# A fused attention and two-layer feed-forward kernel: the second product in seven chunks of 512 tokens

## The chip, the cores and the metric

The kernel runs on one core of a Trainium2 chip. The metric is the device time of one execution in microseconds (us): the median of the runs, and lower is better. The times shown for the kernel before are 1512.82, 1510.32 and 1512.70 us, so the median is 1512.7.

## The reference

Attention over 8 batches, 12 heads, 448 tokens and 64 dimensions, with a root-mean-square norm on queries and keys, and behind it a feed-forward network with h·cos(h) as its activation. All is float32.

```python
def _attn_ref(q, k, v, g_q, g_k):            # each (8, 12, 448, 64)
    q_n, k_n = rmsnorm(q, g_q), rmsnorm(k, g_k)
    scores = scale * np.matmul(q_n, k_n.transpose(0, 1, 3, 2))
    attn = softmax(scores)
    return np.matmul(attn, v)

def _moe_ref(x, w_in, w_out):                # (3584, 768), (768, 2048), (2048, 768)
    h = x @ w_in
    g = h * np.cos(h)
    return g @ w_out

x = attn_out.transpose(0, 2, 1, 3).reshape(8 * 448, 12 * 64)
```

## The kernel before

Everything is kept transposed: features lie on the 128 partitions, tokens along the row. One batch has 448 tokens (`S`), and 8 batches (`B`) make 3584.

The kernel has two parts, each with its own plan. A `Plan` is a list scheduler in the kernel's source: every step is added with its engine, an assumed cost, a due time and the buffers that it reads and writes, and `order()` plays the steps through by these figures and gives the order in which they are issued. On the chip each engine takes its instructions in that order and waits on semaphores for what they need.

The first part does the attention for all batches (two heads at a time), and between its steps the first product, h = x·w_in, for batches 0 to 6 (`multiply`, `ffn1`, lines L545 to L547). There are 16 blocks (`fc`) of 128 rows of h. Each is the sum over six slices of the 768 features, and each slice takes three matmuls, because x and the weights are split into a rounded high part and the rest: high·high, high·low and low·high. So a block is 18 matmuls of 128x128 weights on 448 columns. ScalarE copies a finished block out of PSUM (`h_out`, L557), and SyncE (SP) stores it to DRAM in `h_d` (`h_store`, L560). The weights of the second product are split in the same way and lie in DRAM in `wo_d`.

The second part does the first product of the last batch (`ffn1_block`), and behind it the second product for all batches, one batch of 448 tokens after the other. In the order of the instructions on the chip the last splits of x of the first part (`x_split`, L529 and L531) stand between the first steps of the second part. While the last batch's blocks run, each weight tile of the first product is replaced by one of the second (`v_place`). The second product goes through the 16 blocks of h in pairs (`NG = 2`):

- `gl_load` (L567): SP loads a pair of blocks of one batch from `h_d` into `hb`, 128 x 2 x 448. The ring has 4 buffers.
- `g_turns` (L574 on VectorE, L576 on GpSimd): the whole turns of 2π in h, times -C1. The ring `n` has 2 buffers.
- `g_reduce` (L582, L584 on VectorE): h less these turns. The ring `r2` has 2 buffers.
- `g_cos` (L588, L589 on ScalarE): the absolute value, and the sine of π/2 less it.
- `g_mul` (L593 on VectorE): times h.
- `g_split` (L602 on ScalarE, L600 on GpSimd): the high part and the rest, three buffers each.
- `ffn2` (L616 to L618 on TensorE): for each of the two blocks, into each of six PSUM banks (one for 128 of the 768 output features), three matmuls of 128x128 weights on 448 columns, 18 in all.

A chunk holds its six banks over all 16 blocks. There are eight banks in the ring, so the next chunk starts on the two that are free, and then needs those that were just finished. `y_out` copies a bank to SBUF (ScalarE L630 for even `oc`, VectorE L632 for odd ones, and the very last bank in two halves), and `y_store` (L635) stores it on SP's queue. SBUF slots for these copies are those of `xf`, one for each of the six heads' pairs of the attention part.

Of the kernel before, what the change touches and what calls it, by code (L numbers as in the profile page):

```python
# [10 lines left out]
F32 = mybir.dt.float32  # L11
F32R = mybir.dt.float32r
# [12 lines left out]
PE, ACT, DVE, POOL, SP = "PE", "ACT", "DVE", "POOL", "SP"  # L25


class Plan:
# [18 lines left out]
    def add(self, eng, cost, due, fn, *args, r=(), w=(), land=0.0, start=0.0, lead=None):  # L47
        n = len(self.parts)
        deps = set()
        for key in r:  # L50
            deps.update(self.writer.get(key, ()))
        for key in w:
            deps.update(self.writer.get(key, ()))
            deps.update(self.readers.get(key, ()))
        for key in (*r, *w):
            name, inst = key[0], key[1]
            if name in self.rings:
                self.users.setdefault((name, inst), []).append(n)
        for key in r:
            self.readers.setdefault(key, []).append(n)  # L60
        for key in w:
            self.writer[key] = [n]
            self.readers[key] = []
        deps.discard(n)
        self.parts.append((eng, cost, due, fn, args, deps, land))
        self.start.append(start)
        self.lead.append(self.LEAD * (eng == PE) if lead is None else lead)
# [59 lines left out]
def tile_attention_moe(  # L127
# [11 lines left out]
    nc = tc.nc  # L139
    NU = sd_in.shape[0]  # L140
    B, S, D = 8, kT.shape[2], 64
# [7 lines left out]
    NFC = w_in.shape[0]  # L149
    NOC = 6  # L150
    DM = NCC * 128
    HM = DM // 2
    f64 = w_in.dtype == mybir.dt.int64
    NG = 2


    cpool = ctx.enter_context(tc.tile_pool(name="cpool", bufs=1))
    wpool = ctx.enter_context(tc.tile_pool(name="wpool", bufs=1))
    xpool = ctx.enter_context(tc.tile_pool(name="xpool", bufs=1))
    epool = ctx.enter_context(tc.tile_pool(name="epool", bufs=2))  # L160
    dpool = ctx.enter_context(tc.tile_pool(name="dpool", bufs=1, space=bass.MemoryType.DRAM))
# [4 lines left out]
    ps_o = att.enter_context(tc.tile_pool(name="ps_o", bufs=1, space=PSUM))  # L166
    ps_h = att.enter_context(tc.tile_pool(name="ps_h", bufs=1, space=PSUM))

    h_d = dpool.tile([B, NFC, 128, S], F32, tag="h_d", name="h_d")
    wo_d = dpool.tile([NFC, 128, 2, DM], F32, tag="wo_d", name="wo_d")  # L170
    rk_d = dpool.tile([NU, 128, 7], F32, tag="rk_d", name="rk_d")
    rs_d = dpool.tile([NU, 7, 128], F32, tag="rs_d", name="rs_d")
# [329 lines left out]
    xf = {}  # L502
# [50 lines left out]
    hes = {}  # L553
# [3 lines left out]
        nc.scalar.copy(he, phs.pop((b, fc))[:, :S])  # L557

    def h_store(b, fc):
        nc.sync.dma_start(h_d[b, fc], hes.pop((b, fc)))  # L560


    gts = {}

    def gl_load(b, gi):
        hb = gpool.tile([128, NG, S], F32, tag="hb", name=f"hb{b}_{gi}", bufs=4)
        nc.sync.dma_start(hb, h_d[b, gi * NG : gi * NG + NG].rearrange("f p s -> p f s"))  # L567
        gts[(b, gi)] = {"h": hb}

    def g_turns(b, gi, step):  # L570
        d = gts[(b, gi)]
        if step == 0:
            n = d["n"] = gpool.tile([128, NG, S], F32, tag="n", name=f"n{b}_{gi}", bufs=2)
            nc.vector.tensor_scalar(n, d["h"], 1.0 / (2.0 * math.pi), MAGIC, op0=ALU.mult, op1=ALU.add)  # L574
        else:
            nc.gpsimd.tensor_scalar(d["n"], d["n"], -MAGIC, -C1, op0=ALU.add, op1=ALU.mult)  # L576

    def g_reduce(b, gi, step):
        d = gts[(b, gi)]
        if step == 0:  # L580
            r = d["r"] = gpool.tile([128, NG, S], F32, tag="r2", name=f"r2{b}_{gi}", bufs=2)
            nc.vector.tensor_tensor(r, d["h"], d["n"], ALU.add)  # L582
        else:
            nc.vector.scalar_tensor_tensor(d["r"], d.pop("n"), C2 / C1, d["r"], op0=ALU.mult, op1=ALU.add)  # L584
# [9 lines left out]

    def g_split(b, gi, lo):
        d = gts[(b, gi)]
        t = gpool.tile([128, NG, S], F32R, tag="glo" if lo else "ghi", name=f"g{lo}{b}_{gi}")
        d["lo" if lo else "hi"] = t
        if lo:
            nc.gpsimd.tensor_tensor(t, d.pop("r"), d["hi"].bitcast(F32), ALU.subtract)  # L600
        else:
            nc.scalar.copy(t, d["r"])  # L602

    ys = {}

    def ffn2(b, fc):
        d = gts[(b, fc // NG)]
        hi, lo = d["hi"][:, fc % NG, :], d["lo"][:, fc % NG, :]
        w = wts[("wo", fc)]
        for oc in range(NOC):  # L610
            if fc == 0:
                ys[(b, oc)] = ps_y.tile([128, 512], F32, tag="y", name=f"y{b}_{oc}")
            y = ys[(b, oc)][:, :S]
            whi = w[:, 0, oc * 128 : oc * 128 + 128]
            wlo = w[:, 1, oc * 128 : oc * 128 + 128]
            nc.tensor.matmul(y, whi, hi, start=(fc == 0), stop=False)  # L616
            nc.tensor.matmul(y, whi, lo, start=False, stop=False)  # L617
            nc.tensor.matmul(y, wlo, hi, start=False, stop=(fc == NFC - 1))  # L618

    yes = {}  # L620

    def y_out(b, oc, hf=None):
        y = ys[(b, oc)][:, :S]
        if (b, oc) not in yes:
            yes[(b, oc)] = xpool.tile([128, S], F32, tag=f"xf{oc}", name=f"ye{b}_{oc}")
        ye = yes[(b, oc)]
        if hf is not None:
            y, ye = (t[:, hf * S // 2 : hf * S // 2 + S // 2] for t in (y, ye))
        if (hf if hf is not None else oc) % 2 == 0:
            nc.scalar.copy(ye, y)  # L630
        else:
            nc.vector.tensor_copy(ye, y)  # L632

    def y_store(b, oc):
        nc.sync.dma_start(out[oc * 128 : oc * 128 + 128, b * S : (b + 1) * S], yes.pop((b, oc)))  # L635


    plan = Plan(RING)
    add = plan.add
    ISS, LAND = 0.45, 5.0  # L640
# [159 lines left out]
    def multiply(b):  # L800
        for fc in range(NFC):
            key = ("ph", NSP + NFC * b + fc)
            for part in range(3):
                d = ffn_due(b, 3 * fc + part)
                r = [("w", fc), ("wlo", fc, 0), ("wlo", fc, 1)]
                r += [("xs", cc, s) for cc in (2 * part, 2 * part + 1) for s in range(2)]
                add(PE, 1.215, d, ffn1, b, fc, part, ps_h, "ph", r=r, w=[key])
            add(ACT, 0.53, d - 4, h_out, b, fc, r=[key], w=[("he", NFC * b + fc)])
            add(SP, ISS, d, h_store, b, fc, r=[("he", NFC * b + fc)], land=LAND)
# [22 lines left out]
    gpool = ctx.enter_context(tc.tile_pool(name="gpool", bufs=3, reuse_waits="tile"))  # L832
    ps_y = ctx.enter_context(tc.tile_pool(name="ps_y", bufs=8, space=PSUM, reuse_waits="tile"))
    plan = Plan(RING2)
    add = plan.add
    BLOCK = 3.66

    for fc in range(NFC):
        d = BLOCK * fc
        add(PE, BLOCK, d, ffn1_block, B - 1, fc, w=[("y", fc), ("w", fc)])  # L840
        add(ACT, 0.53, d + 4.0, h_out, B - 1, fc, r=[("y", fc)], w=[("he", fc)])
        add(SP, ISS, d + 5.0, h_store, B - 1, fc, r=[("he", fc)], w=[("hd", B - 1, fc)], land=LAND)
        add(SP, ISS, d + 6.0, v_place, fc, w=[("w", fc)], land=8.0)
    for b in range(B):
        for gi in range(NFC // NG):
            n = (NFC // NG) * b + gi
            d = BLOCK * (NFC * (b + 1) + NG * gi)
            hb, t, r2, hi, lo = (("hb", n), ("n", n), ("r2", n), ("ghi", n), ("glo", n))
            add(SP, ISS, d - 30.0, gl_load, b, gi, r=[("hd", b, NG * gi + i) for i in range(NG)], w=[hb], land=LAND)
            add(DVE, 0.9, d - 20.0, g_turns, b, gi, 0, r=[hb], w=[t])  # L850
            add(POOL, 1.3, d - 19.0, g_turns, b, gi, 1, w=[t])
            add(DVE, 1.1, d - 17.0, g_reduce, b, gi, 0, r=[hb, t], w=[r2])
            add(DVE, 1.8, d - 16.0, g_reduce, b, gi, 1, r=[t], w=[r2])
            add(ACT, 2.0, d - 14.0, g_cos, b, gi, w=[r2])
            add(DVE, 1.12, d - 11.0, g_mul, b, gi, r=[hb], w=[r2])
            add(ACT, 0.95, d - 9.0, g_split, b, gi, 0, r=[r2], w=[hi])
            add(POOL, 2.8, d - 8.0, g_split, b, gi, 1, r=[r2, hi], w=[lo])
            for fc in (NG * gi, NG * gi + 1):
                out_keys = [("y", NFC + NOC * b + oc) for oc in range(NOC)]
                add(PE, BLOCK, BLOCK * (NFC * (b + 1) + fc), ffn2, b, fc, r=[hi, lo, ("w", fc)], w=out_keys)  # L860
        for oc in range(NOC):
            y = ("y", NFC + NOC * b + oc)
            d = BLOCK * NFC * (b + 2) + oc
            if b == B - 1 and oc == NOC - 1:
                add(ACT, 0.3, d - 12.0, y_out, b, oc, 0, r=[y], w=[("ye", oc)])
                add(DVE, 0.35, d - 12.0, y_out, b, oc, 1, r=[y], w=[("yf", oc)])
            else:
                add(DVE if oc % 2 else ACT, 0.62 if oc % 2 else 0.53, d - 12.0, y_out, b, oc, r=[y], w=[("ye", oc)])
            add(SP, ISS, d, y_store, b, oc, r=[("ye", oc), ("yf", oc)], land=LAND)
    with tc.manual_schedule():  # L870
        for f, a in plan.order():
# [48 lines left out]
```

## Time and profile before

| what | value |
|---|---|
| median of the 3 runs shown (lowest, highest) | 1512.7 us (1510.32, 1512.82) |
| span of the profiled execution | 1515.6 us |
| busy: TensorE, its weight loads, VectorE, ScalarE, GpSimd | 1469.8, 1224.4, 1049.0, 874.2, 856.5 us |
| granted TensorE clock, mean | 0.993 |
| matmuls of the second product | 3 lines of 768 |
| DMA traffic | 204.33 MB, mean 135 GB/s |

The profiled execution has no other time of its own than its span, which is 2.9 us (0.2%) over the median. PE is TensorE's matmuls and PEld its weight loads, which run beside them; DVE is VectorE, ACT ScalarE, POOL GpSimd, and SPq the DMA issues of SyncE's queue. Matmuls are pipelined: the recorded duration of one is longer than the distance to the start of the next, and a busy TensorE isn't one at its peak. A wait is put down to the releaser that came last.

### The profile page before, as it was taken

The numbers are of one execution on the slowest core, as the hardware profiler recorded it, in microseconds if no ns is written. First come the engines' busy times: TensorE is split into PE (matmuls) and PEld (weight loads), VectorE is DVE, ScalarE is ACT, GpSimd is POOL, SyncE is SP. The second block draws the span as 40 slices with busy tenths as digits, with TensorE's granted clock in tenths as the row PEclk, the third lists the DMA queues.
The fourth block names the chain that finished last, engine by engine and source line by source line (L and its number), as shares of the span: only waits on it lengthen the run. The fifth ranks groups of instructions, "written<-read, shape, count | busy, mean of one in ns | idle before, by whom it ended". The sixth has DMA issues, their size and how long they took to land.

```text
span 1515.6 us, 22459 instructions
## 1 busy us (share of the span) xinstructions
PE 1469.8 (97%) x7692; PEld 1224.4 (81%) x7692; DVE 1049.0 (69%) x1891; ACT 874.2 (58%) x1763; POOL 856.5 (57%) x694
## 2 busy tenths in 40 slices
PE   7898998999999999999999999999999999999998
PEld 3446787878788878877877788789999999999998
DVE  7878998778777777777776765451566666566561
ACT  5767777677767766766765665441344344344441
POOL 5869788766856655865755552131444444544441
PEclk9999999999999999999999999999999999999999
DMA  6577424555545455544444431296133233233221
GB/s 205 179 217 218 123 82 132 182 177 172 157 155 184 144 152 164 162 147 144 150 153 126 130 118 57 67 310 218 60 100 107 62 97 98 61 99 104 66 74 37
DMA packets 116963, 204.33 MB, mean 135 GB/s; under 512 B 19232, under 2 KB 95856, under 8 KB 116848
## 3 DMA queue, kind: packets, MB, share of 16 engines
q1 hardware_dynamic: 116848, 202.90, 42.9%
q8 instruction: 60, 0.98, 0.3%
q14 instruction: 55, 0.45, 0.1%
HBM read 149.55 MB, written 53.29 MB: 134 GB/s over the span
## 4 chain that ended last, share of the span: by engine, by line
PE 78%; DVE 6%; ACT 3%; issue 3%; POOL 1%; DMA 0%; ACTq 0%; POOLq 0%; DVEq 0%
PE y L616 10%; PE y L618 10%; PE y L617 10%; PE ph L545 9%; PE ph L546 8%; PE ph L547 8%; PE O L500 8%; PE PT L464 7%; PE S L419 6%; ACT hi L475 1%; DVE lo L483 1%; DVE S L426 1%; DVE xf L517 1%; DVE hi L485 1%; ACT P L439 0%
## 5 line engine op out<-in xcount | busy, mean ns | idle before, releaser
L545 PE MATMUL ph<-xs,wi 128*128 128x448 f32 x768 | 299.5, 390 | 3.5 <-ACT he L557 3.5
L546 PE MATMUL ph<-xs,wi 128*128 128x448 f32 x768 | 282.7, 368 | 0.9 <-DVE xs L531 0.9
L547 PE MATMUL ph<-xs,wi 128*128 128x448 f32 x768 | 281.6, 367 | 0.0
L616 PE MATMUL y<-g,wo 128*128 128x448 f32 x768 | 281.1, 366 | 0.0
L618 PE MATMUL y<-g,wo 128*128 128x448 f32 x768 | 280.8, 366 | 0.0
L617 PE MATMUL y<-g,wo 128*128 128x448 f32 x768 | 280.7, 366 | 0.0
L439 ACT ACTIVATE P<-S,sm 128x448 f32<-128x448 f32 x336 | 214.4, 641 | 99.7 <-DVE S L426 88.9
L600 POOL TENSOR_TENSOR g<-r,g 128x896 fp32r<-128x896 f32 x64 | 139.6, 2181 | 184.9 <-ACT g L602 184.9
L426 DVE TENSOR_SCALAR_CACHE_REDUCE S<-S,nr 128x448 f32<-128x448 f32 x336 | 219.4, 683 | 19.0 <-PE S L419 17.5
L475 ACT CAST hi<-PT 128x448 fp32r<-128x448 f32 x336 | 164.8, 536 | 86.5 <-PE PT L464 47.7
L483 DVE TENSOR_TENSOR lo<-PT,hi 128x448 fp32r<-128x448 f32 x252 | 145.3, 617 | 79.7 <-ACT hi L475 78.9
L464 PEld LDWEIGHTS PT<-ident,P 128*128 128x128 f32 x1344 | 158.6, 143 | 33.9 <-issue 22.8
L464 PE MATMUL PT<-ident,P 128*128 128x128 f32 x1344 | 184.2, 278 | 0.1
L545 PEld LDWEIGHTS ph<-xs,wi 128*128 128x128 f32 x768 | 145.2, 189 | 34.9 <-issue 12.9
L547 PEld LDWEIGHTS ph<-xs,wi 128*128 128x128 f32 x768 | 145.0, 189 | 12.5
L616 PEld LDWEIGHTS y<-g,wo 128*128 128x128 f32 x768 | 144.2, 188 | 13.1 <-ACT ye L630 0.7
L546 PEld LDWEIGHTS ph<-xs,wi 128*128 128x128 f32 x768 | 145.5, 189 | 10.9 <-DVE xs L531 1.6
L618 PEld LDWEIGHTS y<-g,wo 128*128 128x128 f32 x768 | 144.2, 188 | 11.9
L617 PEld LDWEIGHTS y<-g,wo 128*128 128x128 f32 x768 | 144.2, 188 | 11.6
L582 DVE TENSOR_TENSOR r<-hb,n 128x896 f32<-128x896 f32 x64 | 93.1, 1455 | 84.9 <-POOL g L600 82.2
L297 POOL TENSOR_TENSOR r<-r,nhalf 128x14 f32<-128x14 f32 (+1 forms) x50 | 127.2, 2545 | 42.8 <-DVE r L293 32.7
L593 DVE TENSOR_TENSOR r<-r,hb 128x896 f32<-128x896 f32 x64 | 73.3, 1146 | 101.8 <-ACT r L589 101.8
(83 smaller groups left out, 2545.2 us busy)
## 6 DMA issues: line engine op xcount, KB each, us to landing
h_d<-he SPq DMA_DIRECT2D x128, 224.0 KB
hb<-h_d SPq DMA_DIRECT2D x64, 448.0 KB
sd<-sd SPq DMA_DIRECT2D x46, 448.0 KB
vd<-v SPq DMA_DIRECT2D x84, 160.0 KB
qd<-qT SPq DMA_DIRECT2D x48, 256.0 KB
raw<-w_in SPq DMA_DIRECT2D x16, 768.0 KB
rawo<-w_out SPq DMA_DIRECT2D x32, 384.0 KB
wo_d<-rawo SPq DMA_DIRECT2D x32, 384.0 KB
```

What stands on the lines that cost most here:

```text
L426: nc.vector.tensor_scalar(d["S", t][:, :S], d["S", t][:, :S], d["nr"][:, t : t + 1], None, op0=ALU.mult, op1=ALU.min, accum_out=d["sm"][:, ...
L439: nc.scalar.activation(tl(u, f"P{t}", [128, S], F32, "P"), d.pop(("S", t))[:, :S], AF.Exp, bias=sm[:, 1, t : t + 1], scale=-1.0, accum_out ...
L464: nc.tensor.transpose(pt[:, t * 128 : t * 128 + 128], src, ident)
L475: nc.scalar.copy(hi, pt[:, hh * S : hh * S + S])
L483: nc.vector.tensor_tensor(lo, src, hi.bitcast(F32), ALU.subtract)
L545: nc.tensor.matmul(ph[:, :S], whi, x2[:, 0, :], start=(cc == 0), stop=False)
L546: nc.tensor.matmul(ph[:, :S], whi, x2[:, 1, :], start=False, stop=False)
L547: nc.tensor.matmul(ph[:, :S], wlo, x2[:, 0, :], start=False, stop=(cc == NCC - 1))
L600: nc.gpsimd.tensor_tensor(t, d.pop("r"), d["hi"].bitcast(F32), ALU.subtract)
L616: nc.tensor.matmul(y, whi, hi, start=(fc == 0), stop=False)
L617: nc.tensor.matmul(y, whi, lo, start=False, stop=False)
L618: nc.tensor.matmul(y, wlo, hi, start=False, stop=(fc == NFC - 1))
```

## The change

The second product takes its tokens in seven chunks (`NT`) of 512 columns (`CT`), not in eight batches of 448. A chunk goes across the borders of batches, and so `h_d` in DRAM is laid out as 16 blocks of 128 rows of 3584 tokens: a store of one batch's block writes 128 pieces of 1792 bytes that lie 14336 bytes apart, and a load reads pieces of 2048 bytes. All tiles of the pair's steps are 512 wide, a matmul fills a whole PSUM bank, and the copies of the result have six slots of their own (`ye`), not those of `xf`. The planner's figures for the second part are changed to fit.

```diff
+    CT = 512
+    NT = B * S // CT
-    h_d = dpool.tile([B, NFC, 128, S], F32, tag="h_d", name="h_d")
+    h_d = dpool.tile([NFC, 128, B * S], F32, tag="h_d", name="h_d")
...
     def h_store(b, fc):
-        nc.sync.dma_start(h_d[b, fc], hes.pop((b, fc)))
+        nc.sync.dma_start(h_d[fc][:, b * S : b * S + S], hes.pop((b, fc)))
...
     def gl_load(b, gi):
-        hb = gpool.tile([128, NG, S], F32, tag="hb", name=f"hb{b}_{gi}", bufs=4)
-        nc.sync.dma_start(hb, h_d[b, gi * NG : gi * NG + NG].rearrange("f p s -> p f s"))
+        hb = gpool.tile([128, NG, CT], F32, tag="hb", name=f"hb{b}_{gi}", bufs=4)
+        nc.sync.dma_start(hb, h_d[gi * NG : gi * NG + NG, :, b * CT : b * CT + CT].rearrange("f p s -> p f s"))
...
-            n = d["n"] = gpool.tile([128, NG, S], F32, tag="n", name=f"n{b}_{gi}", bufs=2)
+            n = d["n"] = gpool.tile([128, NG, CT], F32, tag="n", name=f"n{b}_{gi}", bufs=2)
...
-            r = d["r"] = gpool.tile([128, NG, S], F32, tag="r2", name=f"r2{b}_{gi}", bufs=2)
+            r = d["r"] = gpool.tile([128, NG, CT], F32, tag="r2", name=f"r2{b}_{gi}", bufs=2)
...
-        t = gpool.tile([128, NG, S], F32R, tag="glo" if lo else "ghi", name=f"g{lo}{b}_{gi}")
+        t = gpool.tile([128, NG, CT], F32R, tag="glo" if lo else "ghi", name=f"g{lo}{b}_{gi}")
...
-            y = ys[(b, oc)][:, :S]
+            y = ys[(b, oc)]
...
-            yes[(b, oc)] = xpool.tile([128, S], F32, tag=f"xf{oc}", name=f"ye{b}_{oc}")
+            yes[(b, oc)] = gpool.tile([128, CT], F32, tag=f"ye{oc}", name=f"ye{b}_{oc}", bufs=1)
...
-    BLOCK = 3.66
+    BLOCK, BLOCK2 = 3.66, 4.1
+    D2 = BLOCK * NFC
...
-    for b in range(B):
+    for b in range(NT):
         for gi in range(NFC // NG):
             n = (NFC // NG) * b + gi
-            d = BLOCK * (NFC * (b + 1) + NG * gi)
+            d = D2 + BLOCK2 * (NFC * b + NG * gi)
+            bs = range(b * CT // S, (b * CT + CT - 1) // S + 1)
...
-                add(PE, BLOCK, BLOCK * (NFC * (b + 1) + fc), ffn2, b, fc, r=[hi, lo, ("w", fc)], w=out_keys)
+                add(PE, BLOCK2, D2 + BLOCK2 * (NFC * b + fc), ffn2, b, fc, r=[hi, lo, ("w", fc)], w=out_keys)
```

The assumed costs of the pair's steps change with the width too (for instance L600 on GpSimd from 2.8 to 2.5 us, L602 on ScalarE from 0.95 to 1.08), and so do the widths in `y_out` and `y_store`.

More of the change, by code (lines that the diff above doesn't have):

```diff
@@ L622, in y_out @@
     def y_out(b, oc, hf=None):
-        y = ys[(b, oc)][:, :S]
+        y = ys[(b, oc)]
         if (b, oc) not in yes:
-            yes[(b, oc)] = xpool.tile([128, S], F32, tag=f"xf{oc}", name=f"ye{b}_{oc}")
+            yes[(b, oc)] = gpool.tile([128, CT], F32, tag=f"ye{oc}", name=f"ye{b}_{oc}", bufs=1)
         ye = yes[(b, oc)]
         if hf is not None:
-            y, ye = (t[:, hf * S // 2 : hf * S // 2 + S // 2] for t in (y, ye))
+            y, ye = (t[:, hf * CT // 2 : hf * CT // 2 + CT // 2] for t in (y, ye))
         if (hf if hf is not None else oc) % 2 == 0:
@@ L634, in y_store @@
     def y_store(b, oc):
-        nc.sync.dma_start(out[oc * 128 : oc * 128 + 128, b * S : (b + 1) * S], yes.pop((b, oc)))
+        nc.sync.dma_start(out[oc * 128 : oc * 128 + 128, b * CT : (b + 1) * CT], yes.pop((b, oc)))
     plan = Plan(RING)
@@ L843, in tile_attention_moe @@
         add(SP, ISS, d + 6.0, v_place, fc, w=[("w", fc)], land=8.0)
-    for b in range(B):
+    for b in range(NT):
         for gi in range(NFC // NG):
             n = (NFC // NG) * b + gi
-            d = BLOCK * (NFC * (b + 1) + NG * gi)
+            d = D2 + BLOCK2 * (NFC * b + NG * gi)
+            bs = range(b * CT // S, (b * CT + CT - 1) // S + 1)
             hb, t, r2, hi, lo = (("hb", n), ("n", n), ("r2", n), ("ghi", n), ("glo", n))
[L849 to L857, printed above, removed]
+            add(SP, ISS, d - 30.0, gl_load, b, gi, r=[("hd", bb, NG * gi + i) for i in range(NG) for bb in bs], w=[hb], land=LAND)
+            add(DVE, 1.0, d - 20.0, g_turns, b, gi, 0, r=[hb], w=[t])
+            add(POOL, 1.5, d - 19.0, g_turns, b, gi, 1, w=[t])
+            add(DVE, 1.66, d - 17.0, g_reduce, b, gi, 0, r=[hb, t], w=[r2])
+            add(DVE, 1.3, d - 16.0, g_reduce, b, gi, 1, r=[t], w=[r2])
+            add(ACT, 2.3, d - 14.0, g_cos, b, gi, w=[r2])
+            add(DVE, 1.3, d - 11.0, g_mul, b, gi, r=[hb], w=[r2])
+            add(ACT, 1.08, d - 9.0, g_split, b, gi, 0, r=[r2], w=[hi])
+            add(POOL, 2.5, d - 8.0, g_split, b, gi, 1, r=[r2, hi], w=[lo])
@@ L858, in tile_attention_moe @@
             for fc in (NG * gi, NG * gi + 1):
                 out_keys = [("y", NFC + NOC * b + oc) for oc in range(NOC)]
-                add(PE, BLOCK, BLOCK * (NFC * (b + 1) + fc), ffn2, b, fc, r=[hi, lo, ("w", fc)], w=out_keys)
+                add(PE, BLOCK2, D2 + BLOCK2 * (NFC * b + fc), ffn2, b, fc, r=[hi, lo, ("w", fc)], w=out_keys)
         for oc in range(NOC):
             y = ("y", NFC + NOC * b + oc)
-            d = BLOCK * NFC * (b + 2) + oc
-            if b == B - 1 and oc == NOC - 1:
+            d = D2 + BLOCK2 * NFC * (b + 1) + oc
@@ L865, in tile_attention_moe @@
+            if b == NT - 1 and oc == NOC - 1:
                 add(ACT, 0.3, d - 12.0, y_out, b, oc, 0, r=[y], w=[("ye", oc)])
@@ L867, in tile_attention_moe @@
             else:
-                add(DVE if oc % 2 else ACT, 0.62 if oc % 2 else 0.53, d - 12.0, y_out, b, oc, r=[y], w=[("ye", oc)])
+                add(DVE if oc % 2 else ACT, 0.7 if oc % 2 else 0.6, d - 12.0, y_out, b, oc, r=[y], w=[("ye", oc)])
             add(SP, ISS, d, y_store, b, oc, r=[("ye", oc), ("yf", oc)], land=LAND)
```

## The prediction

> **What bounds the kernel now.** I read the page's busy line, its slices and its chain first, then the second product's part of the trace by windows, then its waits.
>
> ```profile
> span 1515.6 us, 22459 instructions
> PE 1469.8 (97%) x7692; PEld 1224.4 (81%) x7692; DVE 1049.0 (69%) x1891; ACT 874.2 (58%) x1763; POOL 856.5 (57%) x694
> ...
> PE y L616 10%; PE y L618 10%; PE y L617 10%; PE ph L545 9%; PE ph L546 8%; PE ph L547 8%; PE O L500 8%; PE PT L464 7%; PE S L419 6%; ACT hi L475 1%; DVE lo L483 1%; DVE S L426 1%; DVE xf L517 1%; DVE hi L485 1%; ACT P L439 0%
> ...
> L616 PE MATMUL y<-g,wo 128*128 128x448 f32 x768 | 281.1, 366 | 0.0
> ```
>
> TensorE is the bound, and the three lines of the second product (L616 to L618) carry 10% of the chain each. 366 ns is the recorded life of one matmul, not its price: neighbours overlap. The price is the distance from one start to the next, so I take windows of one chunk each (core 0, TensorE alone: us, busy and count, clock, DMA share, GB/s).
>
> ```profile
> 1043.04:1102.56 59.52, 59.52 (x289) 1.00 0.23 71
> 1102.56:1160.94 58.38, 58.38 (x289) 1.00 0.29 93
> 1160.94:1219.32 58.38, 58.38 (x289) 1.00 0.26 82
> ...
> 1453.10:1511.62 58.52, 58.52 (x289) 1.00 0.12 41
> sum 468.58, PE 468.58; mean PE 58.57
> ```
>
> Eight chunks of 288 matmuls (the 289th is the neighbour's), no idle time, full clock: 58.38 / 288 = 202.7 ns a matmul in an ordinary chunk, 59.52 / 288 = 206.7 ns in the first. The stage takes 468.6 us, and almost nothing else is in it. From 1043 us on TensorE's own waits are these:
>
> ```profile
> PEld y L616 <- ACT ye L630: 0.7, 3, 0.2
> ```
>
> That is three stops at chunk borders, where the evacuation of a bank came late. So the stage's time is a count of matmuls times a spacing, and the question is what 512 columns do to the spacing.
>
> **The change part by part.** The count first. 16 blocks x 18 matmuls x 7 chunks = 2016 in place of 2304, 288 fewer. The columns in all are the same, 2016 x 512 = 2304 x 448. Only what a matmul costs beside its columns can be saved.
>
> The price of a column comes from a stretch in which the clock was halved (a window, then the list of instructions in it: start, life).
>
> ```profile
> 125.90:132.60 6.70, 5.76 (x19) 0.50 0.41 123
> ...
> 130.21 0.57 PE L546 MATMUL ph<-xs,wi 128*128 128x448 f32 x1
> ...
> 132.08 0.57 PE L500 MATMUL O<-hi,vs 128*128 128x448 f32 x1
> ```
>
> Five spacings in 132.08 - 130.21 = 1.87 us: 374 ns for 448 columns, 0.835 ns a column at clock 0.50. At full clock that is 187 ns for 448 columns and 213.5 for 512. The measured 202.7 is 16 ns more, and in the first chunk 20 ns more. What are they? They don't come from the next matmul's weight load: a matmul with no load behind it lives as long.
>
> ```profile
> 607.49 0.37 PE L546 MATMUL ph<-xs,wi 128*128 128x448 f32 x1
> 607.49 0.19 PEld L547 LDWEIGHTS ph<-xs,wi 128*128 128x128 f32 x1
> 607.70 0.37 PE L547 MATMUL ph<-xs,wi 128*128 128x448 f32 x1
> 607.99 0.19 PEld L419 LDWEIGHTS S<-khi,qhi 64*128 64x128 f32 x2 [0.31 <-issue]
> ```
>
> The matmul of 607.70 lives its neighbour's 0.37 us, though no load starts in the 0.29 us after it. All matmuls of this form in the trace have 448 columns, so no row shows how the 16 ns go with the width. Bounds: they vanish in a longer stream (spacing 213.5), they stay (229.5), or they grow with the columns (202.7 x 512/448 = 231.6). I take the fixed one, 229.5: two spacings stand in the trace for the same 448 columns, 202.7 and 206.7, so the excess follows something other than the columns, and at half clock the spacing grows 1.85 times, not twice, so it doesn't run on the array's clock. The rows leave the third nearly as open, at 2 ns from it. Sum: 2016 x 229.5 = 462.7 us against 468.6: **-5.9**.
>
> A rule to weigh here: the Trainium skill's "TensorE: Matmul & The Clock Gate", section "Back-to-back issue gap", gives N / 2.4 + 2.5 ns for a warm matmul, which is 189 ns at 448 columns and 216 at 512. The trace disagrees at 448 by 14 ns; by the rule at 512 alone, the estimate for the stage is 435 us. The section "Wait — 56ns, not 53.3ns?" of that page says that the fixed part does not show on the cold array; the 374 ns agree.
>
> Elementwise work on h, in groups of the steady stage (mean ns after the busy time):
>
> ```profile
> L600 POOL TENSOR_TENSOR g<-r,g 128x896 fp32r<-128x896 f32 x53 | 114.4, 2159 | 131.6 <-ACT g L602 131.6
> L582 DVE TENSOR_TENSOR r<-hb,n 128x896 f32<-128x896 f32 x51 | 76.0, 1491 | 48.0 <-POOL g L600 48.0
> L576 POOL TENSOR_SCALAR n<-n 128x896 f32<-128x896 f32 x50 | 67.4, 1347 | 71.0 <-DVE n L574 69.3
> L593 DVE TENSOR_TENSOR r<-r,hb 128x896 f32<-128x896 f32 x52 | 59.7, 1149 | 81.1 <-ACT r L589 81.1
> L584 DVE SCALAR_TENSOR_TENSOR r<-n,r 128x896 f32<-128x896 f32 x52 | 56.8, 1092 | 1.8
> ...
> L574 DVE TENSOR_SCALAR n<-hb 128x896 f32<-128x896 f32 x50 | 43.6, 872 | 1.6
> ```
>
> Each step runs 56 times in place of 64, on 1024 columns in place of 896. Per pair of blocks VectorE needs 1.49 + 1.15 + 1.09 + 0.87 = 4.6 us and GpSimd 2.16 + 1.35 = 3.5, under the 7.3 us (36 x 202.7 ns) of TensorE; times 8/7 that is 5.3 and 4.0, under 8.3. Cost 0; the cover is TensorE's 3 us of slack a pair on VectorE.
>
> DMAs. SP issues 56 loads of 512 KB for 64 of 448 KB and 42 stores of the result of 256 KB for 48 of 224 KB: 14 issues fewer, the same bytes, at a DMA share of 0.12 to 0.29. Cost 0 under TensorE. The 128 stores of h keep size and number; their rows of 1792 bytes now lie 14336 bytes apart. Who waits for h and for its stores:
>
> ```profile
> L560 SPq DMA_DIRECT2D h_d<-he x128: 319/327/585, 132.9 to 1043.8; - x128
> ...
>   DVE n L574: 14.5, 4
>   ACT he L557: 6.8, 3
> ...
> ACT he L557 <- DMA h_d<-he: 6.8, 3, 3.5
> ```
>
> ScalarE waits three times for a store of h in the whole run, 6.8 us, and the last row, from the waits of 965 to 1060 us alone, has all three; eight banks of PSUM stand there between it and TensorE. Price between 0 and 6.8, I take 0. Chunk 0 reads h of the first two batches and the last chunk that of the last two, all stored long before except the last. The result's copies leave the slots of xf for six slots of their own, each refilled one chunk later: 0.
>
> The change of stage. These pieces of the chain stand between TensorE's two products:
>
> ```profile
> 982.39 0.54 ACT he L557
> 982.94 0.02 issue
> 982.96 0.61 DVE xs L531
> 983.57 1.00 DVE r L584
> 984.57 1.49 DVE xs L531
> ```
>
> The first pair's elementwise step (L584) sits between two splits of x that TensorE waits for. At 8/7 it costs 0.14 us more, with the step before it 0.3. **+0.3**. If the order turns there, the whole 1.00 could leave or another 1.5 come in.
>
> Borders: six in place of seven. The copies grow 8/7, and so does TensorE's time to the first bank in use. Before they cost at most the 0.7 us above; after the same: 0.
>
> The end:
>
> ```profile
> 1511.82 0.39 DVE L632 COPY ye<-y 128x224 f32<-128x224 f32 x1 [0.59 <-PE y L618]
> 1512.24 0.35 ACT L630 COPY ye<-y 128x224 f32<-128x224 f32 x1 [0.51 <-DVE ye L632]
> ...
> 1511.40:1515.60 4.20, 0.38 (x2) 0.00 (x0) 0.39 (x1) 0.68 (x2) 0.00 (x0) 0.94 0.63 230
> ```
>
> Two half copies in turn, 32 columns more in each (0.05 us each at most), and a last store with 32 KB more at 230 GB/s (0.14): **+0.2**.
>
> Sum: -5.9 + 0.3 + 0.2 = -5.4 us, a span of 1510.2. The span is 2.9 us over the median of the runs shown (1512.7), so the forecast for the median is **1507.3**.
>
> **The rivals.**
> - The excess goes with the columns. For it: rows show one width only, and a stream that stutters evenly would be hidden at half clock too. Against: two spacings for the same columns. The Trainium skill's "SBUF — State Buffer", "Specifications (TRN2)", gives 16-byte lines with a penalty for each crossing, which would be such a stutter; no run here shows it. 2016 x 231.6 = 466.9, -1.7 + 0.5: 1511.5, no change.
> - The excess vanishes in the longer stream. For it: at half clock nothing of it is left to see. Against: it is there at 448 in a matmul without a load behind it. 2016 x 213.5 = 430.4, -38.2 + 0.5: 1475.0. (By the clock gate page's rule above it would be 1480.)
> - The slower spacing of the first chunk, 20 ns over the columns, holds in all chunks. It ended in the trace at the first border and never came back. 2016 x 233.5 = 470.7, +2.1 + 0.5: 1515.3.
> - Slower than before: that spacing, and it grows with the columns: 206.7 x 8/7 = 236.2, 476.2 us, +7.6 + 0.5: 1520.8. From a spacing of 233.7 on (468.6 + 3 - 0.5 over 2016) the change is a loss that can be measured.
> - Stores and loads of h now share rows in DRAM. Between 974 and 1044 us SP's one queue holds the loads of chunk 0, the last batch's stores and the weights; a store held until a load has landed would hold all behind it. A load took 977.79 - 974.10 = 3.7 us to its first reader (below). Sixteen such holds less eight banks of cover: about 8 x 1.5 = 12 us, 1520. Against it: the two touch different columns.
>
> ```profile
> 974.10 0.43 SPq L567 DMA_DIRECT2D hb<-h_d  x1
> ...
> 977.79 0.63 DVE L574 TENSOR_SCALAR n<-hb 128x896 f32<-128x896 f32 x1 [3.43 <-DMA hb<-h_d]
> ```
>
> **How the numbers follow.** Fixed excess 0.55 (faster), excess gone 0.09 (faster), excess by columns 0.17 (same), slow spacing with fixed excess 0.08 (same), slow spacing by columns 0.06 and the held queue 0.05 (slower). About 0.2%, 3 us, is what a measurement can tell here: the three runs span 2.5 us. Faster 0.64, same 0.25, slower 0.11. The range leaves out the excess gone (0.09), the slow spacing by columns and the held queue (0.11). Its top is the slow fixed case, 1515.3, with 0.7 for the stage change. Its bottom: the shortest matmuls of the stage live 3 ns less than the median,
>
> ```profile
> L616 PE MATMUL y<-g,wo x768: 362/365/472, 1043.0 to 1511.0; 128*128 128x448 f32 x192
> ```
>
> so all of them at 226.5 give 456.6 us, 6 less than the forecast: 1501, and 1.5 for the L584 step of the stage change: 1499.5. The likeliest case alone: 1500 to 1510.
>
> **What would show it.** Right: windows of one chunk hold 288 matmuls in about 66.1 us, full clock, and TensorE's waits in the stage stay under 1 us; VectorE's L582 near 1.7 us and GpSimd's L600 near 2.5, both with idle time before them. Wrong by the columns: 66.7 us and more; wrong by the vanished excess: 62.2. Wrong by the stage change: the first L616 not near 1043 us, or "ACT he" waiting for its stores by far more than 6.8 us. The planner's figure for a block in the diff, 4.1 us (228 ns a matmul), sets its order and is no measurement of mine.

## The result, and the profile after

The changed kernel takes 1502.5 us (median of 4 runs, 1500.2 to 1506.5), the kernel before 1512.05 (median of 4, with one run more than the table has). The ratio is 0.9938, with a 95% interval of 0.992 to 0.9955: 9.6 us faster, by 0.6%. The forecast was 1507.3.

The page of the changed kernel, its first lines and one of the three lines of the second product:

```profile
span 1500.1 us, 21753 instructions
...
PE 1453.1 (97%) x7404; PEld 1164.9 (78%) x7404; DVE 1036.8 (69%) x1856; ACT 867.3 (58%) x1736; POOL 848.5 (57%) x678
...
L618 PE MATMUL y<-g,wo 128*128 128x512 f32 x672 | 262.5, 391 | 0.0
```

TensorE executes 288 matmuls fewer (7404 for 7692). Windows of one chunk each, TensorE alone (us, busy and count, clock, DMA share, GB/s):

```profile
1037.80:1103.10 65.30, 65.30 (x289) 1.00 0.26 79
1103.10:1168.40 65.30, 65.30 (x289) 1.00 0.29 84
1168.40:1234.00 65.60, 65.60 (x290) 1.00 0.30 88
...
1430.50:1496.10 65.60, 65.60 (x289) 1.00 0.12 42
sum 458.30, PE 458.30; mean PE 65.47
```

65.30 / 288 = 226.7 ns a matmul, in the first chunk too. The stage takes 458.3 us for 468.6: **-10.3**. Chunks three to seven take 0.2 to 0.3 us more than the first two; these are stops at the borders. The waits that TensorE's weight loads show in the stage (total us, times, longest):

```profile
PEld y L618 <- ACT ye L632: 1.3, 5, 0.3
PEld y L618 <- DVE ye L634: 1.3, 5, 0.3
```

Ten stops for the three of before. The 2.6 us are idle time of the weight loads, which run ahead; in the starts of the matmuls each stop is about 0.1 us, 1.0 us for all ten. Work of both products and copies otherwise runs beside TensorE, as before.

The two spans differ by more, 1515.6 - 1500.1 = 15.5 us. 5.2 of them lie ahead of the second product, which starts at 1037.8 us for 1043.0. A window in the attention part, all engines (busy time of TensorE, its weight loads, VectorE, ScalarE, GpSimd), kernel before:

```profile
245.00:260.00 15.00, 12.96 (x61) 9.88 (x60) 11.82 (x27) 8.74 (x20) 14.64 (x12) 0.77 0.52 148
```

and the changed kernel:

```profile
245.00:260.00 15.00, 11.59 (x63) 8.51 (x62) 13.00 (x31) 11.93 (x28) 14.92 (x13) 1.00 0.46 137
```

The granted clock is 0.77 in this window before, with a stretch at 0.50 in it (248.8 to 255.4 us), and 1.00 after. Such stretches fall differently in each execution: the version with chunks of 448 below (the third experiment) started its second product at 1039.0 us, and the changed kernel in a later profile at 1041.8. So the 5.2 us are no saving of the change; the medians, taken over several executions, show 9.6 us.

### The profile page after: what moved, and what is told of

It reads as the page before. It is cut to its first block, busy times and chain, and to the rows that moved or that the text cites. A ratio compares the mean times of both kernels' runs of the same rounds, so it can differ in the third digit from the quotient of the medians.

```text
span 1500.1 us, 21753 instructions
## 1 busy us (share of the span) xinstructions
PE 1453.1 (97%) x7404; PEld 1164.9 (78%) x7404; DVE 1036.8 (69%) x1856; ACT 867.3 (58%) x1736; POOL 848.5 (57%) x678
## 4 chain that ended last, share of the span: by engine, by line
PE 77%; DVE 6%; ACT 3%; issue 3%; POOL 2%; DMA 1%; ACTq 0%; POOLq 0%; DVEq 0%
PE y L618 10%; PE y L619 10%; PE y L620 10%; PE ph L547 9%; PE ph L548 8%; PE ph L549 8%; PE O L502 8%; PE PT L466 7%; PE S L421 6%; ACT hi L477 1%; DVE lo L485 1%; DVE S L428 1%; DVE xf L519 1%; DVE hi L487 1%; DVE wo L217 1%
## 5 line engine op out<-in xcount | busy, mean ns | idle before, releaser
L618 PE MATMUL y<-g,wo 128*128 128x512 f32 x672 | 262.5, 391 | 0.0
L620 PE MATMUL y<-g,wo 128*128 128x512 f32 x672 | 261.5, 389 | 0.0
L619 PE MATMUL y<-g,wo 128*128 128x512 f32 x672 | 261.5, 389 | 0.0
L428 DVE TENSOR_SCALAR_CACHE_REDUCE S<-S,nr 128x448 f32<-128x448 f32 x336 | 219.4, 684 | 17.6 <-PE S L421 16.1
L602 POOL TENSOR_TENSOR g<-r,g 128x1024 fp32r<-128x1024 f32 x56 | 140.9, 2516 | 156.1 <-ACT g L604 156.0
L590 ACT ACTIVATE r<-r 128x1024 f32<-128x1024 f32 x56 | 59.4, 1061 | 167.7 <-DVE r L586 167.5
L584 DVE TENSOR_TENSOR r<-hb,n 128x1024 f32<-128x1024 f32 x56 | 83.6, 1493 | 103.6 <-POOL g L602 102.3
L618 PEld LDWEIGHTS y<-g,wo 128*128 128x128 f32 x672 | 126.1, 188 | 28.7 <-ACT ye L632 1.3
L578 POOL TENSOR_SCALAR n<-n 128x1024 f32<-128x1024 f32 x56 | 76.7, 1370 | 125.7 <-DVE n L576 124.6
L620 PEld LDWEIGHTS y<-g,wo 128*128 128x128 f32 x672 | 126.1, 188 | 26.3
```

The costliest lines, as they stand in the source:

```text
L428: nc.vector.tensor_scalar(d["S", t][:, :S], d["S", t][:, :S], d["nr"][:, t : t + 1], None, op0=ALU.mult, op1=ALU.min, accum_out=d["sm"][:, ...
```

## The experiments

Three theories of the gain stood at the start. All take 288 matmuls less; they differ in what a matmul costs beside its columns. *Fixed*: the same at every width. *Columns*: it grows with them. *Fall*: it depends on how the width or the row's start falls, so that 448 can be a bad width. A fourth rival was that the gain sits in the other parts of the change.

**1. Widths by themselves** (e1_widths). A kernel with bursts of matmuls alone, one line for each form; it ran once:

```diff
+        for h, oc, y, cs, _ in turns():          # 180 matmuls
+            nc.tensor.matmul(y[:, :480], w[:, cs], x[:, h, 0:480], start=True, stop=True)
...
+            nc.tensor.matmul(y[:, :512], wb[:, cs], xb[:, h, 0:512], start=True, stop=True)   # bfloat16
```

> Leaves out attention and both products: it is only bursts of 180 matmuls, one burst for each form, with nothing that TensorE waits for. The 128x128 weights and the moving operand are rounded float32 as in the second product, with 512, 448 (rows of 448), 448 (rows of 512), 480, 416, 384, 320, 256 columns and 448 from column 64 on; then 512 and 448 with 64 columns of weights, bfloat16 at 512 and 448, plain float32 at 512 and 448, and 512 again. In the kernels 512 columns took 226.7 ns from start to start, 448 took 202.7 or 206.7; at 0.417 ns a column that leaves 13.3 and 16 or 20 ns. Theory A, a fixed excess of about 13 to 16 ns whatever the width: 480 gives 213 to 216, 416 187 to 189, 384 173 to 176, 320 147 to 149, 256 120 to 123 ns. Theory B, the excess grows with the columns (0.443 ns a column from the 512 case): 480 gives 212.5, 416 184, 384 170, 320 142, 256 113. Theory C, the excess depends on how the width or the row's start falls (512 falls well, 448 badly): 448 from rows of 512 gives 200.0 if it is the start of the row; if it is the width, 384 and 256 stand at 13.3 (173.3 and 120.0) and 480, 416 and 320 at 16 to 20 ns over their columns. If it is a matter of rounded float32 alone, bfloat16 shows another excess at the same width; if the weight load makes it, half as many weight columns change it.

The bursts by line (life in ns: min, median, max; first and last start in us; shape):

```profile
L49 PE MATMUL y<-z,w x180: 362/365/369, 50.0 to 86.3; 128*128 128x448 f32 x180
L51 PE MATMUL y<-x,w x180: 362/365/369, 86.5 to 122.8; 128*128 128x448 f32 x180
L53 PE MATMUL y<-x,w x180: 374/378/382, 123.0 to 161.8; 128*128 128x480 f32 x180
L55 PE MATMUL y<-x,w x180: 347/348/350, 162.0 to 195.4; 128*128 128x416 f32 x180
L57 PE MATMUL y<-x,w x180: 333/334/346, 195.6 to 226.6; 128*128 128x384 f32 x180
L59 PE MATMUL y<-x,w x180: 303/309/309, 226.8 to 253.1; 128*128 128x320 f32 x180
L61 PE MATMUL y<-x,w x180: 281/283/283, 253.2 to 274.7; 128*128 128x256 f32 x180
L65 PE MATMUL y<-x,w x180: 387/391/398, 311.3 to 352.5; 128*64 128x512 f32 x180
L69 PE MATMUL y<-xb,wb x180: 379/379/390, 389.1 to 427.7; 128*128 128x512 bf16 x180
L71 PE MATMUL y<-xb,wb x180: 352/352/353, 428.0 to 461.8; 128*128 128x448 bf16 x180
```

The distance of the first and the last start over 179 is the spacing, to 0.6 ns. 256 columns: 21.5 us / 179 = 120.1. Against 512 in the kernel (226.7) that is 106.6 ns for 256 columns, 0.4165 a column, and what is left is 13.4 ns at both ends. In between: 320 13.6, 384 13.3, 416 13.3, 448 16.2, 480 16.8. So *fixed* holds at 13.3 for most of these widths, and the width part of *Fall* holds for the rest: a hump on top near 450 to 480. *Columns* (113 ns at 256) falls. The start of the row does nothing: L49 and L51 differ in the row's length alone and take the same. bfloat16 leaves 2 to 3 ns at both widths (215.6 and 188.8), so the 13 ns come with rounded float32; weights and moving operand changed their type together there, and which of the two it is was not tried.

**2. The layout alone** (e2_layout_only), on the kernel before:

```diff
-    h_d = dpool.tile([B, NFC, 128, S], F32, tag="h_d", name="h_d")
+    h_d = dpool.tile([NFC, 128, B * S], F32, tag="h_d", name="h_d")
...
-        nc.sync.dma_start(h_d[b, fc], hes.pop((b, fc)))
+        nc.sync.dma_start(h_d[fc][:, b * S : b * S + S], hes.pop((b, fc)))
...
-        nc.sync.dma_start(hb, h_d[b, gi * NG : gi * NG + NG].rearrange("f p s -> p f s"))
+        nc.sync.dma_start(hb, h_d[gi * NG : gi * NG + NG, :, b * S : b * S + S].rearrange("f p s -> p f s"))
```

> The kernel before with the change's layout of h in DRAM alone: stores of 1792-byte rows 14336 bytes apart, chunks still of 448 tokens. Theory that the whole gain is the second product's spacing and count: ratio 1.000 to the kernel before, within 0.2%, second product 468 us. Rival, the layout helps or costs by itself (other row pitch, SP's queue held in the change of stage): a ratio of 0.997 or 1.003 or beyond, and a start of the second product that moves by 3 us or more.

Ratio 0.9993, interval 0.998 to 1.0005: no gain or cost that can be measured. But its second product was 2 us longer than that of the kernel before. Four of its eight chunks, and what TensorE waited for in the stage:

```profile
1041.86:1100.20 58.34, 58.34 (x289) 1.00 0.24 72
1100.20:1160.00 59.80, 59.80 (x290) 1.00 0.30 92
1219.40:1277.80 58.40, 58.40 (x290) 1.00 0.31 92
1453.00:1512.50 59.50, 59.50 (x290) 1.00 0.11 39
```

```profile
PEld y L616 <- ACT ye L630: 0.5, 2, 0.2
PEld y L616 <- DVE ye L632: 0.3, 1, 0.3
```

The slow spacing of 206.7 ns, which the kernel before has in its first chunk, is here in the second, third and last. Inside the second product it changes only within the first 13 matmuls of a chunk.

**3. The changed kernel with 448 columns** (e3_after_448):

```diff
-    CT = 512
+    CT = 448
...
-    BLOCK, BLOCK2 = 3.66, 4.1
+    BLOCK, BLOCK2 = 3.66, 3.66
```

> The changed kernel with chunks of 448 again (eight of them; the planner's block 3.66 us, its other new costs, the new layout and the result's own slots stay). Width theory: the second product takes 466.9 to 468.6 us again (spacing 202.7), ratio to the kernel before 1.000 within 0.2%. Rival, the gain sits in the other parts of the change (layout, slots of the result, planner's costs): the ratio stays near 0.994.

Ratio 0.9997, interval 0.9985 to 1.001. The width is the whole gain; the layout, the result's own slots and the planner's other new costs give none that can be measured. This version has no stops in its stage, and all eight chunks are at 202.7 ns:

```profile
1039.00:1097.40 58.40, 58.40 (x290) 1.00 0.24 71
1447.60:1505.90 58.30, 58.30 (x289) 1.00 0.12 42
```

**4. More widths** (e4_more_widths), bursts as in the first, with 192 and 128 columns, fewer weight columns, the same weights three times in a row, and sums into one bank. It ran once.

> Again only bursts of 180 matmuls in rounded float32, without attention and products: 512, 496, 464, 448, 432, 400, 352, 288, 192 and 128 columns on 128 weight columns; 448 and 512 columns on 32 weight columns; 384 and 256 on 64; 448 with the same weights for three in a row; 448 into one PSUM bank as sums of six; and 448 with each sixth matmul at 256 columns. The first bursts gave 13.3 ns over the columns at 256, 320, 384, 416 and 512, 16.0 at 448 and 16.7 at 480 in an uneven pattern. Theory, a floor of 13.3 for every width of 256 or more and an uneven pattern on top at some widths: 496, 464, 432, 400, 352 and 288 stand at 13.3 to 20; none is under 13.3. Rival, it is smooth around 450 to 480 (a hump): 464 about 16.3, 432 about 14.7, 496 about 15. At 192 and 128 the weight load should show: its part was 107 ns where it wasn't hidden (293 against 187 ns), so about 120 ns at both. If the uneven pattern comes from the weight load, 32 weight columns change it and the same weights for three in a row don't (each matmul still loads); if it comes from the PSUM side, one bank changes it.

```profile
L49 PE MATMUL y<-x,w x180: 382/382/383, 49.5 to 88.8; 128*128 128x496 f32 x180
L51 PE MATMUL y<-x,w x180: 367/372/376, 89.1 to 126.6; 128*128 128x464 f32 x180
L55 PE MATMUL y<-x,w x180: 352/359/365, 163.3 to 198.4; 128*128 128x432 f32 x180
L57 PE MATMUL y<-x,w x180: 341/341/353, 198.6 to 230.8; 128*128 128x400 f32 x180
L59 PE MATMUL y<-x,w x180: 320/323/326, 231.0 to 259.9; 128*128 128x352 f32 x180
L61 PE MATMUL y<-x,w x180: 292/294/296, 260.0 to 283.6; 128*128 128x288 f32 x180
L63 PE MATMUL y<-x,w x180: 248/273/278, 283.7 to 303.7; 128*128 128x192 f32 x180
L65 PE MATMUL y<-x,w x180: 243/276/277, 303.8 to 323.8; 128*128 128x128 f32 x180
L67 PE MATMUL y<-x,w x180: 362/363/368, 323.9 to 360.1; 128*32 128x448 f32 x180
L73 PE MATMUL y<-x,w x180: 276/276/279, 433.1 to 453.4; 128*64 128x256 f32 x180
L75 PE MATMUL y<-x,w x180: 362/365/369, 453.6 to 489.8; 128*128 128x448 f32 x180
L77 PE MATMUL y<-x,w x180: 362/365/369, 490.0 to 526.3; 128*128 128x448 f32 x180
```

Over the columns at 0.4167 ns each: 496 12.9, 464 16.2, 432 16.1, 400 13.2, 352 14.8, 288 11.8. The hump spans 432 to 480 and ends at 400 and at 496; 352 stands 1.5 over the 13.3 by itself. The theory had said that nothing lies under 13.3; 288 does, by 1.5. At 192 and 128 columns the spacing stops falling, at 20.0 us / 179 = 111.7 ns, which fits the weight load of 107 ns; no burst had a smaller load at these widths. At 448, a quarter of the weight columns (L67: 202.2), the same weights (L75: 202.2) and one bank for all (L77: 202.8) leave the spacing as it is: neither the size of the load nor the PSUM side makes the hump there. With each sixth matmul at 256 columns the mean is 33.8 us / 179 = 188.8 ns, which is what five of 202.7 and one of 120.1 give. At 256 the size does count: with half the weight columns (L73) the spacing is 20.3 us / 179 = 113.4 ns for 120.1, and only 6.7 of the 13.3 are left. So the 13.3 isn't one cost that every matmul pays whatever stands beside it.

**5. Fourteen chunks of 256** (e5_after_256): `CT = 256`, `BLOCK2 = 2.16` and the costs to fit.

> The changed kernel with fourteen chunks of 256 columns, the planner's costs scaled to fit. Theory, count times (columns + 13.3 ns): 4032 matmuls of 120 ns are 483.8 us against 458 us, about 26 us slower than the changed kernel, near 1528 us. Rival, the time goes with the columns: no change against the changed kernel. Rival, VectorE or ScalarE bound the pair there (their fixed cost per instruction doubles in number): TensorE waits show in the stage and the time lies above 1535.

1655.2 us, ratio 1.093 (1.0911 to 1.0948). The spacing came out at the 120 ns of the theory, but the time at that of the third expectation: from the third chunk's end on TensorE stops in each pair, for GpSimd's split (L602). Its row at a stop and rows of the pair's steps on the other engines, then the waits of the stage and all 112 executions of one step (min, median, max):

```profile
1149.69 1.76 POOL L602 TENSOR_TENSOR g<-r,g 128x512 fp32r<-128x512 f32 x1
1150.37 1.63 DVE L586 SCALAR_TENSOR_TENSOR r<-n,r 128x512 f32<-128x512 f32 x1
...
1151.51 0.39 PE L619 MATMUL y<-g,wo 128*128 128x256 f32 x1 [1.14 <-POOL g L602]
...
1152.10 0.63 ACT L590 ACTIVATE r<-r 128x512 f32<-128x512 f32 x1 [2.96 <-DVE r L586]
...
1153.52 0.69 DVE L595 TENSOR_TENSOR r<-r,hb 128x512 f32<-128x512 f32 x1 [1.51 <-ACT r L591]
...
1154.71 0.62 POOL L578 TENSOR_SCALAR n<-n 128x512 f32<-128x512 f32 x1 [3.25 <-DVE n L576]
...
1156.09 1.63 DVE L586 SCALAR_TENSOR_TENSOR r<-n,r 128x512 f32<-128x512 f32 x1
```

```profile
PE y L619 <- POOL g L602: 102.8, 90, 1.4
```

```profile
L586 DVE SCALAR_TENSOR_TENSOR r<-n,r x112: 691/1632/1669, 975.2 to 1637.0; 128x512 f32<-128x512 f32 x112
```

Two steps are long: L586 on VectorE takes 1.63 us for 512 columns, where it took 1.09 for 896 in the kernel before, and L602 on GpSimd takes 1.76, where 8/14 of 2.16 would be 1.23. It is not the width that makes them so. L586 stays at 0.69 us in nearly all of its executions that don't overlap L602, most of them in the first chunks, and is at 1.63 in the median of those that do. Nor is an engine full, as the expectation had it: from 1200 to 1600 us VectorE is busy for 61% of the time, ScalarE for 36%, GpSimd for 42%, and a pair's steps add up to 3.4 us on VectorE and 2.4 on GpSimd, under TensorE's 36 x 120 = 4.3 us. What takes 1156.09 - 1150.37 = 5.7 us a pair is one chain: L586, then L590 and L591 on ScalarE, L595 and the next pair's L576 on VectorE, L578 on GpSimd, L584 and L586 on VectorE again, each about as soon as the one before it is done. The planner had taken L586 for 0.68 us and L602 for 1.3. Another order was not tried.

**6 to 10. The borders.** The first and the last block of a chunk are given to the planner in six parts, so that a bank's copy is planned when that bank is done and not when all six are:

```diff
...
+                if fc in (0, NFC - 1):
+                    for oc in range(NOC):
+                        add(PE, BLOCK2 / NOC, D2 + BLOCK2 * (NFC * b + fc + oc / NOC), ffn2, b, fc, (oc,), lead=0.0, r=[hi, lo, ("w", fc)], w=out_keys[oc : oc + 1])
+                    continue
```

The changed kernel ran unchanged beside it:

> The changed kernel again, unchanged, beside the others: ratio to the kernel before 0.992 to 0.9955, a spacing of 226.7 ns in all chunks, about ten stops of 105 ns at the chunk borders.

> The changed kernel with the first and the last block of a chunk given to the planner in six parts, one for each bank, so that a finished bank's copy is planned as soon as that bank is done. Theory, the ten stops at the borders cost 1.0 us and come from copies that stand behind other work: stops gone, the second product 457.1 us for 458.1; in the whole time at most 0.1%, not to be told from none. Rival: the finer order moves the pair's steps and opens other waits, the time grows by 0.2% or more.

The changed kernel: 0.9928 (0.9914 to 0.9941), its stage 458.0 us from first to last start. With the new borders: 0.9904 (0.9889 to 0.9919), 456.8 us and no stop; all its chunks are like the first:

```profile
1039.10:1104.40 65.30, 65.30 (x289) 1.00 0.26 81
```

The stage says 1.2 us, the two medians of that call 4. So both ran again, and the same borders on the kernel before:

> The kernel before (chunks of 448) with the first and last block of a chunk planned in six parts, as in the borders version of the changed kernel. Theory, the second spacing at 448 columns (206.7 ns) is taken up or left where TensorE stops at a border: without stops one spacing holds through the whole second product, 202.7 ns (466.9 us) or 206.7 (476.2 us) in all eight chunks. Rival, the spacing changes by itself: it changes inside the stage without a stop before it. Ratio to the kernel before 0.998 to 1.004.

> The borders version of the changed kernel once more. Theory: 1.2 us under the changed kernel, the stops' price, ratio to the kernel before 0.9915 to 0.9925. Rival: more than the stops, 0.9905 or below again.

> The changed kernel beside it: ratio to the kernel before 0.9925 to 0.9940.

With borders 0.9922 (0.9907 to 0.9937), without 0.9937 (0.9922 to 0.9952); the stage is 456.7 and 458.0 again. The trace's 1.2 us is repeatable; the two medians of the second call lie 1.3 us apart, and the intervals overlap in both calls, so a gain beyond it isn't shown. The borders version is the fastest that ran, at 1499.4 and 1501.8 us. On the kernel before, the new borders gave 0.9987 (0.9975 to 0.9999), no stop and one spacing, 202.7 ns, in all eight chunks; the first:

```profile
1042.04:1100.40 58.36, 58.36 (x289) 1.00 0.24 74
```

Experiments 3 and 8 have no stop in the second product and hold 202.7 all through it. But stops are not what decides it. In the kernel before the return from 206.7 to 202.7 comes within the first 13 matmuls of the second chunk, and in experiment 2 within the first 13 of the fourth; no two starts lie further apart than 207 and 212 ns there, so there is no stop. The three stops of the kernel before change nothing. The slow spacing does set in right behind a stop at both places of experiment 2, but a third stop of that run changes nothing. So the rival that was named for experiment 8, a change without a stop before it, is in the traces of these two kernels, and what makes the change is open. The changed kernel has the slow spacing too, in its last matmuls of 448 columns: 270 of the first product, without a stop, up to the start of the second product.

```profile
982.00:1037.80 55.80, 55.80 (x271) 1.00 0.96 338
```

That is 206.7 ns, and the 512 columns right behind it take 226.7.

## Why the prediction was right, and where its size was off

- **Count and columns.** Right: 2016 matmuls, full clock, no idle time, and 0.4167 ns a column (0.835 / 2 = 0.4175 was read from the half clock, and the 213.5 of the sum is 512 x 0.417).
- **The excess: the term that was mis-sized.** "I take the fixed one, 229.5" meant 16 ns at 512 columns as at 448. What is the same at 512 and at most other widths is 13.3; the 16 of 448 contains a hump of 2.7 that 512 hasn't, and the prediction had no term for it. The sum by what was measured: before 2304 x 202.7 = 467.0, the first chunk's slow spacing 1.15 and the stops 0.3; after 2016 x 226.7 = 457.0 and the stops 1.0. Fewer matmuls at 13.3 give 288 x 13.3 = 3.8 us of the gain, the hump 2304 x 2.7 = 6.2, the slow spacing 1.15; the stops take 0.7 back. More than half of the gain is that 448 was a bad width. That is luck for the prediction: with the 16.7 ns of 480 columns the stage would have come out near the forecast's 462.7, and the bottom of the range, 226.5 ns a matmul, was taken from the spread of recorded lives, which has nothing to do with the hump. The slow first chunk was luck of the execution: experiments 3 and 8 at 448 columns don't have it, and against their 466.7 us the stage gains 8.7.
- **The weight load.** That the 16 ns don't come from it was read from a matmul's recorded life, whose end is modelled, and a life isn't a spacing. The bursts bear the reading out at 448 columns (202.2 ns with a quarter of the weight columns), but not at 256 (113.4 for 120.1 with half).
- **Elementwise steps, cost 0.** Right, with GpSimd's split at the 2.5 us that were forecast and VectorE's step at 1.53 for 1.7. Means of the steady stage:

```profile
L602 POOL TENSOR_TENSOR g<-r,g 128x1024 fp32r<-128x1024 f32 x45 | 111.7, 2483 | 104.2 <-ACT g L604 104.2
...
L584 DVE TENSOR_TENSOR r<-hb,n 128x1024 f32<-128x1024 f32 x44 | 67.3, 1529 | 68.2 <-POOL g L602 68.2
```

  A sum of busy times under TensorE's isn't enough, though: in experiment 5 it was under, and the chain of the steps was not.
- **DMAs and layout, cost 0.** Right (experiment 2). ScalarE's waits for stores of h rose from 6.8 to 18.4 us in eight waits, which the prediction had named as a sign of being wrong. TensorE didn't feel them: its own waits for ScalarE's copies of h in the first product are 3.5 us before and 3.2 after.
- **Change of stage, +0.3.** Right. From the start of the 5000th matmul to the second product 82.7 us before and 82.9 after, both with the slow spacing in the first product's last blocks. The order did turn: two steps of the first pairs stand between the splits of x (`xs`) now, each at 1.14 us, for one of 1.00.

```profile
975.05 1.14 DVE r L584
...
978.22 1.14 DVE r L586
979.35 1.49 DVE xs L533
```

- **Borders, 0.** Wrong by 0.7 us: ten stops for three. The step said that the copies grow as TensorE's time to the first bank grows; it left out that the planner takes all six banks as done at once, and puts the copies behind other work. Planning them bank by bank took the stops away (experiments 7 to 9). Experiment 3 has no stops without that, so it also hangs on the order that the planner finds. Counted as waits of the weight loads the stops are 2.6 us, over the 1 us that the prediction gave as a sign of being right.
- **The end, +0.2.** 4.2 us from the last matmul's start to the end in both: 0.
- **The rivals.** By columns (231.6) and vanished (213.5) fall to 226.7 and to the bursts. At 512 columns the slow spacing shows in none of the three profiles of the changed kernel, though in the first of them the 448 columns just before have it. The queue wasn't held.

The sum of what moved is -10.3 + 0.3, and the medians moved by 9.6. The terms that are worked out above from the spacings give -10.4 for the -10.3; the rest is rounding.

## What to carry to other kernels

Where TensorE has no idle time, multiply the matmuls by the distance of their starts, not by their recorded lives, and ask what that distance holds beside the columns. Measure the spacing of the widths that the shape allows in a burst by themselves before a loop is laid out: a few per cent hang on the choice, and they need not run evenly with the width. A wider tile pays only as far as the elementwise work beside it stays covered. Compare with TensorE's time not only each engine's sum of busy times, but also the chain of one tile's steps in the order in which they are issued, with the times that they take beside one another: at 256 columns the sums fitted and the chain didn't.

## What the runs showed of the hardware

- In the bursts and kernels here a matmul of rounded float32 with 128 weight columns costs about 13.3 ns over its columns (0.4167 ns each) at 256, 320, 384, 400, 416, 496 and 512 columns, about 16 to 17 from 432 to 480, 14.8 at 352 and 11.8 at 288; bfloat16 costs 2 to 3 at 448 and 512. The rule of the Trainium skill's "TensorE: Matmul & The Clock Gate", section "Back-to-back issue gap" (N / 2.4 + 2.5 ns, given there for an isolated matmul), agrees with the bfloat16 bursts: 215.6 and 188.8 for its 215.8 and 189.2. It does not hold for rounded float32. What makes the 13 ns, and what the hump, stays open: at 448 columns the size of the weight load, the weights' repetition, the bank and the row's start were tried and don't change the spacing by more than 0.5 ns. At other widths the weight load's size does show: 64 weight columns take 41.2 us / 179 = 230.2 ns at 512, 3.5 more than 128, and 113.4 at 256, 6.7 less.
- 448 columns have two spacings, 202.7 and 206.7 ns, and keep one of them for tens of microseconds. It can change without a stop of TensorE. 512 columns showed one, in five profiles.
- With 128 weight columns the spacing is 111.7 ns at 192 as at 128 columns. That the weight load sets it there fits its 107 ns and was not tried by itself.
- A step of VectorE and one of GpSimd side by side can each be far longer than alone: L586 on 512 columns takes 0.69 us alone and 1.63 in the median beside L602 (experiment 5).
